# A tile's splits directly behind the next first layer, the inverse's halves ahead of the product, the row's square behind the second layer, and an earlier table

## The chip, the cores and the metric

The program runs on one core of one Trainium2 chip. The metric is the time on the device in microseconds (us). Five engines run their own queues in order: PE (TensorE; its weight loads are listed apart as PEld), DVE (VectorE), ACT (ScalarE), POOL (GpSimd) and SP (SyncE, which only issues DMAs here). An instruction that waits holds everything behind it on its own engine, and nothing on the others.

## What is computed

Cut to what matters, the reference is a chain of three layers over 8 x 3072 tokens of 256 features:

```python
y = irfft(rfft(x, axis=1) * F, n=3072)            # a long convolution, per feature
h = y @ w_in                                      # 256 -> 1024, the "first layer"
e = exp(h - max(h)); s = h * e / (sum(e) + 1e-9)  # the product h * e is "solu"
z = ((s - mean(s)) / sqrt(var(s) + 1e-6) * g_ln) @ w_out   # 1024 -> 256, the "second layer"
xn, en = z / (|z| + 1e-6), emb / (|emb| + 1e-6)
expert = argmax(xn @ en.T / tau); gate = softmax(xn @ en.T / tau)[expert]
out = gate * (relu(z @ w1[expert]) @ w2[expert])  # 8 experts, 256 -> 1024 -> 256
```

## The kernel before

**Stages.** The FFT is split as 64 x 48 over four passes of two batch rows each; its forward half (`fft`) runs one pass ahead of the rest. Stage B (`stage_b`) is a loop of 192 tiles of 128 tokens, 48 per pass, with the FFT of the next pass threaded through it as small units: `aux(.., 0)` behind the second layer, `aux(.., 1)` at the end of an iteration. In the last pass there is no FFT left, and the units split the expert weights instead (`w_split`, one ACT and one DVE instruction each). Stage C (`stage_c`) runs 128- or 256-token blocks of one expert each.

**What sets the order.** Nothing is reordered after it is written: each engine runs its instructions in the order in which the Python code issues them, with waits where data or a buffer asks for one.

**One iteration i of stage B**, in the order written, with j = i - 3:

- top: tile i-1 is split in two fp16 halves. Even tiles, and all 48 of the last pass, by `turn`: 8 transposes on PE (L936) write the tile's product `es` into its own first-layer PSUM tile `h`, ACT copies it to `T` (L939, the high half), DVE subtracts (L940, the low half). Odd tiles of the first three passes by `send`: ACT and DVE make the halves `hl` in place (L946, L947) and `post` sends them through a transposing DMA on SP one iteration later.
- ACT: `es` = exp (L967); DVE: the product `es` = h * cc * es (L968), which needs `cc` from POOL (L928, L929; the tiles are named `gcc`, `nm` and so on in the traces).
- even i: `inv4`, the fourth FFT stage, for two tiles: PE (L740) into a PSUM tile `a`, then its halves `xh` by ACT (L745) and `xl` by DVE (L746); both are written to the tile `xh`.
- `half`: last iteration's output rows, scaled by `c2` (ACT L1013, DVE L1014).
- the second layer of tile j: 24 matmuls (L983) into `o`.
- `aux(.., 0)`; the first layer of tile i+1 (L758, 12 matmuls); `top(i+1)`: DVE takes the maximum (L925) and `nm` (L926), POOL makes `cc`.
- ACT: the square of `es` into the junk tile `jk` (L995, for the variance); then the row's square, of `o` of tile j (L1001, for the norm), which POOL turns into `c2` (L1009).
- `aux(.., 1)`; then small steps of `b_final`, which routes a group of eight tiles to experts.

There are two `h` tiles in PSUM, so the first layer of tile i+1 overwrites the `h` of tile i-1 and has to wait until DVE's L940 of tile i-1 has read it. There are two `a` tiles, shared by the FFT units and `inv4`.

**Routing.** `b_final` runs a group's norm, softmax and positions as a generator, one step per iteration. Most groups are "slow": their long run of POOL operations (the loop of L808 to L811) is cut in several steps; the last groups run it in one go. One group's state (`snap`) is kept for an early table of the first 24 expert blocks (`first_slots`), whose first slot is gathered (L1169 on POOL) and transposed (L1174 on SP) before stage B ends.

## Time and profile before

| | us |
|---|---|
| median of 3 runs | 2745.77 (2744.71 to 2745.79) |
| the profiled execution | 2744.74 |
| its span, first to last instruction | 2742.9 |
| PE busy | 2620.9 (96%) |
| DVE busy | 1891.5 (69%) |
| ACT busy | 1527.3 (56%) |
| POOL busy | 1328.7 (48%) |

The busy times are over the whole span. Stage B lies between about 193 and 1683 us, stage C behind it. In the chain that ended last PE holds 39% and POOL 20% of the span. A wait in brackets behind a row is the idle time of that engine just before the instruction, with the instruction that ended it.

### The profile page before, as it was taken

How to read it: one execution, taken by the hardware profiler on the slowest of the kernel's cores; microseconds unless marked ns; L12 is line 12 of the kernel's file. 1: busy time of each engine (PE TensorE's matmuls, PEld its weight loads, DVE VectorE, ACT ScalarE, POOL GpSimd, SP SyncE). 2: the span in 40 equal slices, each digit the busy share in tenths (PEclk: the TensorE clock that was granted, in tenths of full speed). 3: DMA queues.
4: the chain of work that ended last, by engine and by line, in shares of the span. 5: the costliest groups of instructions: out<-in, count | busy, mean ns of one | idle time of the engine just before them, and what ended most of it. 6: DMA issues, size and time to landing. Idle time of an engine off the chain costs nothing.

```text
span 2742.9 us, 53684 instructions
## 1 busy us (share of the span) xinstructions
PE 2620.9 (96%) x20090; PEld 2024.3 (74%) x20090; DVE 1891.5 (69%) x2971; ACT 1527.3 (56%) x2852; POOL 1328.7 (48%) x2627
## 2 busy tenths in 40 slices
PE   5889999999999999999999998999999999999998
PEld 4447666676666776666776777888888888888897
DVE  4846899868989769888788975454545454454565
ACT  2556788767877767777688863223333333333332
POOL 2000346545566446665555556644444544454444
PEclk7999999999999999999999999999999999999999
DMA  9768888799997989885344422332323332322222
GB/s 313 202 193 244 222 199 199 195 246 209 195 194 161 234 222 198 191 169 138 94 122 122 126 51 56 74 76 73 79 74 78 76 76 77 77 77 76 78 60 57
DMA packets 444118, 384.13 MB, mean 140 GB/s; under 512 B 284779, under 2 KB 366837, under 8 KB 440784
## 3 DMA queue, kind: packets, MB, share of 16 engines
q1 hardware_dynamic: 391200, 310.34, 48.0%
q0 software_dynamic: 26896, 57.21, 6.8%
q10 hardware_dynamic: 25760, 13.14, 1.9%
q8 instruction: 159, 2.61, 0.4%
q14 instruction: 103, 0.84, 0.1%
HBM read 195.67 MB, written 103.09 MB: 109 GB/s over the span
## 4 chain that ended last, share of the span: by engine, by line
PE 39%; issue 23%; POOL 20%; DVE 12%; DMA 4%; ACT 1%; POOLq 0%; SPq 0%; ACTq 0%; DVEq 0%
PE h L758 15%; PE o L983 11%; POOL crow L1169 7%; POOL out_dram L166 6%; POOL scr L165 3%; DVE nm L925 3%; PE a L514 2%; PE a L688 2%; PE h L936 2%; PE a L740 2%; POOL gcc L928 2%; DMA bufA<-out 1%; DVE T L940 1%; DVE in L586 1%; PE a L650 1%
## 5 line engine op out<-in xcount | busy, mean ns | idle before, releaser
L983 PE MATMUL o<-wo_h,T 128*128 128x264 f16 x3072 | 549.6, 276 | 0.1
L928 POOL TENSOR_SCALAR gcc<-nm 128x1 f32<-128x1 f32 x192 | 180.3, 939 | 725.3 <-DVE nm L926 485.7
L758 PE MATMUL h<-win_h,xh 128*128 128x512 f16 x1536 | 492.4, 382 | 35.1 <-DVE T L940 33.5
L1212 PE MATMUL o<-cw,chh 128*128 128x256 f16 x3152 | 522.7, 273 | 0.8 <-issue 0.8
L1245 PEld LDWEIGHTS <-cw 128*128 128x128 f16 x5184 | 471.0, 98 | 58.1 <-issue 8.3
L983 PEld LDWEIGHTS <-T 128*128 128x128 f16 x4608 | 451.0, 98 | 64.4 <-ACT rows L1001 0.3
L758 PEld LDWEIGHTS <-xh 128*128 128x128 f16 x2304 | 222.0, 98 | 317.1 <-issue 84.8
L166 POOL DMA_INDIRECT out_dram<-cot,ids x197 | 215.2, 1092 | 452.9 <-ACT cot L1215 440.6
L1212 PE MATMUL o<-cw,chl 128*128 128x256 f16 x1576 | 429.7, 273 | 3.8 <-DVE chl L1249 3.6
L983 PE MATMUL o<-wo_l,T 128*128 128x264 f16 x1536 | 423.9, 276 | 0.0
L1249 DVE SCALAR_TENSOR_TENSOR chl<-h,chh 128x512 f16<-128x512 f32 x197 | 134.6, 683 | 389.9 <-ACT chh L1248 373.3
L925 DVE TENSOR_REDUCE nm<-h 128x1 f32<-128x1024 f32 x192 | 234.5, 1221 | 150.8 <-PE h L758 150.4
L1212 PEld LDWEIGHTS <-chh 128*128 128x128 f16 x3152 | 307.4, 98 | 36.7 <-issue 1.4
L1215 ACT ACTIVATE cot<-o,fac 128x256 f32<-128x256 f32 x197 | 93.5, 475 | 413.3 <-PE o L1212 407.6
L1201 DVE COPY cw<-wexp 128x4096 f16 x216 | 275.2, 1281 | 41.1 <-PE o L1212 20.7
L1245 PE MATMUL h<-cxT,cw 128*128 128x256 f16 (+1 forms) x2592 | 292.1, 264 | 7.2 <-DMA cxT<-crow 7.1
L758 PE MATMUL h<-win_l,xh 128*128 128x512 f16 x768 | 293.1, 382 | 0.0
L1245 PE MATMUL a<-cxT,cw 128*128 128x256 f16 (+1 forms) x2592 | 291.7, 263 | 0.4 <-issue 0.4
L968 DVE SCALAR_TENSOR_TENSOR es<-h,gcc,es 128x1024 f32<-128x1024 f32 x192 | 245.7, 1280 | 37.0 <-POOL gcc L929 31.9
L967 ACT ACTIVATE es<-h,nm,isc_h 128x1024 f32<-128x1024 f32 x192 | 230.2, 1199 | 31.3 <-DVE nm L926 19.4
L995 ACT ACTIVATE jk<-es 128x1024 bf16<-128x1024 f32 x192 | 202.1, 1052 | 64.2 <-DVE es L968 63.0
L166 POOL DMA_INDIRECT lst<-gdi,gix x192 | 218.1, 1136 | 35.3 <-issue 33.0
(261 smaller groups left out, 4368.7 us busy)
## 6 DMA issues: line engine op xcount, KB each, us to landing
wst<-in_w_dram SPq DMA_DIRECT2D x128, 256.0 KB
in<-in_x_dram SPq DMA_DIRECT2D x48, 512.0 KB
in<-bufA SPq DMA_DIRECT2D x64, 384.0 KB
c<-bufC SPq DMA_DIRECT2D x96, 256.0 KB
xs<-rows SPq DMA_DIRECT2D x96, 256.0 KB
ft<-in_filt_dram SPq DMA_DIRECT2D x24, 960.0 KB
bufA<-out SPq DMA_DIRECT2D x72, 256.0 KB
zw<-z SPq DMA_DIRECT2D x96, 192.0 KB
```

The lines of the kernel that those rows point to most:

```text
L166: ins = self.nc.gpsimd.indirect_dma_start(in_offset=None, **kw).ins
L758: nc.tensor.matmul(h[:, nb, :], l[:, i, db, :], r[:, db, sl], start=k == 0, stop=k == 5)
L925: nc.vector.tensor_reduce(x[:, 0:1], L["h"], axis=AX.X, op=ALU.max, negate=True)
L928: nc.gpsimd.tensor_scalar(cc, nm, nm, 1.0, op0=ALU.mult, op1=ALU.max)
L967: nc.scalar.activation(L["s"], L["h"], AF.Exp, bias=L["nm"], scale=self.isc_h[:, i // N2:i // N2 + 1], accum_out=col(i, "st", 0))
L968: nc.vector.scalar_tensor_tensor(L["s"], L["h"], col(i, "cc", 0), L["s"], op0=ALU.mult, op1=ALU.mult, accum_out=col(i, "st", 1))
L983: nc.tensor.matmul(o[:, :D + E], T[:, l, :], r[:, f, :], start=q == 0, stop=q == 23)
L995: nc.scalar.activation(jk, L["s"], AF.Square, accum_out=col(i, "st", 2))
L1169: nc.gpsimd.indirect_dma_start(out=rows[:, h, :], out_offset=None, in_=self.xs, in_offset=bass.IndirectOffsetOnAxis(ap=tab["ids"][:, h, k: ...
L1201: nc.vector.tensor_copy(w.rearrange("p (o k) -> p o k", o=1), self.wexp[:, bass.ds(e, 1), part * 4096:(part + 1) * 4096])
L1212: nc.tensor.matmul(o[:, :D], l[f // fs][:, f % fs, h * 128:(h + 1) * 128], w2[:, r, f, :], start=q == 0, stop=q == 23)
L1245: nc.tensor.matmul(t[:, i, :], w1[:, l, db, f * 128:(f + 1) * 128], xT[:, r + db, :n], start=q == 0, stop=q == 5)
```

## The change

Six edits in `stage_b`, and two in what goes with it:

1. `turn` and `send` of tile i move from the top of iteration i+1 to the end of iteration i, behind `jk` and ahead of `aux(.., 1)`. The tiles that go one way or the other stay the same.
2. `inv4`'s work of an even iteration is written ahead of the product L968 and behind the exponential.
3. The row's square and POOL's `c2` move directly behind the second layer, ahead of `aux(.., 0)`, the first layer and `jk`.
4. `first_slots` starts three iterations sooner, from tile 182 and no longer 185, on the state of group 19 and no longer 20; group 19 therefore runs its POOL operations in one go, too.
5. What is left of `b_final` in stage C stops once ahead of its matmul (the state 2), where it ran on before.
6. Two of the twelve transfer matrices that the FFT keeps from its first pass lie in buffers of the tag `wst` and no longer `mt`.

No arithmetic is added or removed, and no instruction: each engine has the same instructions before and after.

```diff
@@ -897,9 +897,7 @@
 
         def over(f, x):
 
-            while x in (2, 3):
-                x = next(f)
-            return x
+            return next(f) if x == 3 else x
 
         src = self.inv4(xp, ps)
         next(src)
@@ -959,17 +957,14 @@
         for i in range(n + LAG):
             j = i - LAG
             now = 0 <= i < n
-            if 0 <= i - 1 < n and i != n - 1:
-                (turn if i % 2 or i > n - N2 else send)(i - 1)
             if now:
                 L = live[i]
                 L["s"] = L["pool"].tile([128, FF], F32, name="es", tag="es")
                 nc.scalar.activation(L["s"], L["h"], AF.Exp, bias=L["nm"], scale=self.isc_h[:, i // N2:i // N2 + 1], accum_out=col(i, "st", 0))
-                nc.vector.scalar_tensor_tensor(L["s"], L["h"], col(i, "cc", 0), L["s"], op0=ALU.mult, op1=ALU.mult, accum_out=col(i, "st", 1))
-            if i == n - 1:
-                turn(i - 1)
             if i % 2 == 0:
                 xs.append(next(src, None))
+            if now:
+                nc.vector.scalar_tensor_tensor(L["s"], L["h"], col(i, "cc", 0), L["s"], op0=ALU.mult, op1=ALU.mult, accum_out=col(i, "st", 1))
             if half:
                 half()
                 half = None
@@ -984,6 +979,12 @@
                         q += 1
                 self.spot = o[:, 272:344]
                 finals = [(f, next(f) if x == 2 else x) for f, x in finals]
+                n2, c2 = col(j, "n2", 0), col(j, "cc", 1)
+                g, k = groups[j // G], j % G
+                if k % 2 == 0:
+                    rows = gp.tile([128, 2, RD], I32, name="rows", tag="rows", bufs=2)
+                nc.scalar.activation(rows[:, k % 2, :].bitcast(BF16)[:, :D], o[:, :D], AF.Square, accum_out=n2)
+                nc.gpsimd.tensor_scalar(c2.bitcast(I32), n2.bitcast(I32), -0.5, float(MAGIC + (8 << 23)), op0=ALU.mult, op1=ALU.add)
             if now:
                 if 0 < i <= n - N2 and i % 2 == 0:
                     post(i - 1)
@@ -993,12 +994,7 @@
                     top(i + 1)
                 jk = L["pool"].tile([128, FF], BF16, name="jk", tag="jk")
                 nc.scalar.activation(jk, L["s"], AF.Square, accum_out=col(i, "st", 2))
-            if 0 <= j < n:
-                n2, c2 = col(j, "n2", 0), col(j, "cc", 1)
-                g, k = groups[j // G], j % G
-                if k % 2 == 0:
-                    rows = gp.tile([128, 2, RD], I32, name="rows", tag="rows", bufs=2)
-                nc.scalar.activation(rows[:, k % 2, :].bitcast(BF16)[:, :D], o[:, :D], AF.Square, accum_out=n2)
+                (turn if i % 2 == 0 or i >= n - N2 else send)(i)
             if now:
                 aux(*divmod(i, N2), 1)
             if puts:
@@ -1006,7 +1002,6 @@
             if 0 <= j < n:
                 nc.vector.tensor_copy(g["raw"][:, k, :], o[:, D:D + E])
                 finals = [(f, next(f) if x == 3 else x) for f, x in finals]
-                nc.gpsimd.tensor_scalar(c2.bitcast(I32), n2.bitcast(I32), -0.5, float(MAGIC + (8 << 23)), op0=ALU.mult, op1=ALU.add)
 
                 def half(j=j, k=k, o=o, c2=c2, rows=rows):
                     rw = rows[:, k % 2, :].bitcast(F16)
@@ -1022,12 +1017,11 @@
 
                 if k == G - 1:
                     p, nn = divmod(j - (G - 1), N2)
-                    finals.append((self.b_final(groups.pop(j // G), p, nn, gp, ps, j // G == n // G - 4, j // G < n // G - 4), 0))
-            if i >= n - N2 + SPLIT + LAG:
+                    finals.append((self.b_final(groups.pop(j // G), p, nn, gp, ps, j // G == n // G - 5, j // G < n // G - 5), 0))
+            if i >= n - N2 + SPLIT:
                 next(early, 0)
             finals = [(f, x) for f, x in ((f, next(f, 1)) for f, _ in finals) if x != 1]
         self.spot = None
-        finals = [(f, over(f, x)) for f, x in finals]
         for _ in early:
             pass
         yield
@@ -1098,7 +1092,7 @@
         ins = nc.gpsimd.indirect_dma_start(
             out=li[:K].rearrange("p k o -> p (k o)"), out_offset=None, in_=self.lst.rearrange("(b k) o -> b (k o)", k=blk),
             in_offset=bass.IndirectOffsetOnAxis(ap=ri[:K].bitcast(U32), axis=0)).ins
-        assert len(self.scattered["lst"]) >= (self.np_run * N2 // G - (3 if start is None else 0)) * G
+        assert len(self.scattered["lst"]) >= (self.np_run * N2 // G - (4 if start is None else 0)) * G
         for name in self.scattered["lst"]:
             self.tc.add_manual_dep(ins, name, mybir.DependencyInfo(mybir.DependencyClass.Sync, mybir.DependencyReason.DATA), reason="the whole list")
         for _ in range(3 if start is None else 7):
@@ -1314,7 +1308,7 @@
                     self.m1 = [x[:, k:k + 4, :] for x in spare for k in (0, 4)]
                     for pool, tag in ((xp, "c4"), (xp, "xh"), (gp, "rows")):
                         self.m1 += [pool.tile([128, 4, 128], F32, name=tag, tag=tag, bufs=2) for _ in range(2)]
-                    self.m1 += [ap.tile([128, 4, 128], F32, name="mt", tag="mt", bufs=3) for _ in range(2)]
+                    self.m1 += [ap.tile([128, 4, 128], F32, name="wst", tag="wst", bufs=3) for _ in range(2)]
                     for _ in self.fft(0, ap, ps, hp):
                         next(prep, 0)
                     for _ in prep:
```

**DVE, an even tile of the second pass.** The rows below are DVE's queue around the product of tile 76. `nm` is the tile's maximum, `y` an FFT unit, `graw` the routing logits, `hl` the low half of tile 75, `xh` the low half of the inverse's output, `es` the product. Before:

```order
L925 TENSOR_REDUCE nm<-h 128x1
L926 TENSOR_SCALAR nm<-nm,isc_h 128x1
L600 TENSOR_TENSOR y<-z,ft 96x1024
L1007 COPY graw<-o 128x8
L947 TENSOR_TENSOR hl<-es,hl 128x1024
L968 SCALAR_TENSOR_TENSOR es,gst<-h,gcc,es 128x1024
L746 SCALAR_TENSOR_TENSOR xh<-a,ysc,xh 128x512
L1014 SCALAR_TENSOR_TENSOR rows<-o,gcc,rows 128x256
```

After:

```order
L923 TENSOR_REDUCE nm<-h 128x1
L924 TENSOR_SCALAR nm<-nm,isc_h 128x1
L945 TENSOR_TENSOR hl<-es,hl 128x1024
L600 TENSOR_TENSOR y<-z,ft 96x1024
L1003 COPY graw<-o 128x8
L746 SCALAR_TENSOR_TENSOR xh<-a,ysc,xh 128x512
L967 SCALAR_TENSOR_TENSOR es,gst<-h,gcc,es 128x1024
L1009 SCALAR_TENSOR_TENSOR rows<-o,gcc,rows 128x256
```

The low half of tile 75 moved from behind the FFT unit and the logits to directly behind `nm`, and the inverse's half from behind the product to ahead of it.

**DVE, the odd tile that follows.** `T` is the low half of tile 76; `gd`, `go`, `goh`, `grc` and `gy` are steps of `b_final`. Before:

```order
L925 TENSOR_REDUCE nm<-h 128x1
L926 TENSOR_SCALAR nm<-nm,isc_h 128x1
L608 TENSOR_TENSOR y<-y,zw 96x1024
L1007 COPY graw<-o 128x8
L840 SCALAR_TENSOR_TENSOR gd<-gd,cst 128x64
L842 TENSOR_REDUCE go_8494<-gd 128x8
L843 TENSOR_TENSOR goh<-gd,go_8494 128x64
L802 RECIPROCAL grc<-gcc 128x8
L803 TENSOR_SCALAR gy<-gV 128x16
L940 TENSOR_TENSOR T<-h,T 128x1024
L968 SCALAR_TENSOR_TENSOR es,gst<-h,gcc,es 128x1024
```

After:

```order
L923 TENSOR_REDUCE nm<-h 128x1
L924 TENSOR_SCALAR nm<-nm,isc_h 128x1
L938 TENSOR_TENSOR T<-h,T 128x1024
L608 TENSOR_TENSOR y<-y,zw 96x1024
L1003 COPY graw<-o 128x8
L840 SCALAR_TENSOR_TENSOR gd<-gd,cst 128x64
L842 TENSOR_REDUCE go_8505<-gd 128x8
L843 TENSOR_TENSOR goh<-gd,go_8505 128x64
L802 RECIPROCAL grc<-gcc 128x8
L803 TENSOR_SCALAR gy<-gV 128x16
L967 SCALAR_TENSOR_TENSOR es,gst<-h,gcc,es 128x1024
```

The low half of tile 76 moved ahead of the FFT unit, the logits and all steps of `b_final`.

**ACT, between the same two products.** `jk` is the square of the product, `rows,gn` the row's square, `z` and `out` are FFT copies, `T` is the high half of tile 76. Before:

```order
L651 ACTIVATE z<-a 96x512
L995 ACTIVATE jk,gst<-es 128x1024
L1001 ACTIVATE rows,gn_7975<-o 128x256
L695 ACTIVATE out<-a 96x512
L839 ACTIVATE gpe<-gd 128x64
L939 ACTIVATE T<-h 128x1024
L967 ACTIVATE es,gst<-h,nm,isc_h 128x1024
```

After:

```order
L986 ACTIVATE rows,gn_7978<-o 128x256
L651 ACTIVATE z<-a 96x512
L996 ACTIVATE jk,gst<-es 128x1024
L937 ACTIVATE T<-h 128x1024
L695 ACTIVATE out<-a 96x512
L839 ACTIVATE gpe<-gd 128x64
L963 ACTIVATE es,gst<-h,nm,isc_h 128x1024
```

The row's square went ahead of the FFT copy and of `jk`, and the high half ahead of the unit `out` and the exponential of `b_final`.

## Rows read from the trace of the kernel before

**Rows 1.** Busy time by stretch: us, length, then busy us of each engine, clock, DMA.

```profile
310.30:347.70 37.40, 33.98 (x204) 21.86 (x202) 33.17 (x46) 26.85 (x51) 11.77 (x26) 0.95 0.79 203
347.70:518.30 170.60, 164.89 (x1040) 108.51 (x1038) 158.08 (x248) 135.60 (x257) 97.44 (x201) 1.00 0.82 192
1392.50:1559.20 166.70, 160.99 (x1181) 117.59 (x1179) 147.36 (x270) 134.71 (x257) 90.75 (x259) 1.00 0.47 124
```

**Rows 2.** Whom PE waited for, whole span: total us, times, longest us.

```profile
PE h L758 <- DVE T L940: 33.5, 33, 2.9
...
PE h L1245 <- DMA cxT<-crow: 7.1, 1, 7.1
PE a L650 <- DVE xh L746: 4.4, 4, 2.1
PE a L514 <- DVE xh L746: 3.6, 3, 1.6
...
PE a L688 <- DVE xh L746: 3.1, 3, 1.2
...
PE a L851 <- DVE goh L843: 2.1, 1, 2.1
```

**Rows 3.** The same, from 193.5 to 1338.5 us alone.

```profile
PE h L758 <- DVE T L940: 24.6, 22, 2.9
```

**Rows 4.** Timeline around one wait: start us, us, engine, line, tiles.

```profile
811.13 1.03 ACT L939 ACTIVATE T<-h 128x1024 f16<-128x1024 f32 x1
...
812.04 0.21 DVE L926 TENSOR_SCALAR nm<-nm,isc_h 128x1 f32<-128x1 f32 x1
...
814.17 1.22 DVE L940 TENSOR_TENSOR T<-h,T 128x1024 f16<-128x1024 f32 x1
...
815.44 0.38 PE L758 MATMUL h<-win_h,xh 128*128 128x512 f16 x1 [0.79 <-DVE T L940]
```

**Rows 5.** Timeline: a slow POOL operation and what DVE ran meanwhile.

```profile
803.20 1.21 DVE L600 TENSOR_TENSOR y<-z,ft 96x1024 f32<-96x1024 f32 x1
...
803.39 2.40 POOL L928 TENSOR_SCALAR gcc<-nm 128x1 f32<-128x1 f32 x1 [1.96 <-DVE nm L926]
...
804.40 1.21 DVE L947 TENSOR_TENSOR hl<-es,hl 128x1024 f16<-128x1024 f32 x1
```

**Rows 6.** Groups by line: busy us, mean ns | idle us before them.

```profile
L968 DVE SCALAR_TENSOR_TENSOR es<-h,gcc,es 128x1024 f32<-128x1024 f32 x192 | 245.7, 1280 | 37.0 <-POOL gcc L929 31.9 <-ACT es L967 3.1
...
L1013 ACT ACTIVATE rows<-o,gcc 128x256 f16<-128x256 f32 x192 | 91.1, 475 | 52.4 <-POOL gcc L1009 43.5 <-POOL scr L165 7.9 <-DVE gpos L861 0.4
```

**Rows 7.** Timeline of an even tile of the last pass.

```profile
1375.64 0.71 ACT L462 ACTIVATE wexp<-wst,sc_w 128x512 f16<-128x512 f32 x1
...
1378.81 0.69 ACT L745 ACTIVATE xh<-a,ysc 128x512 f16<-128x512 f32 x1
...
1380.29 0.75 DVE L746 SCALAR_TENSOR_TENSOR xh<-a,ysc,xh 128x512 f16<-128x512 f32 x1
...
1382.92 1.04 PE L936 MATMUL h<-cst,es 128*128 128x128 f32 x8
```

**Rows 8.** Timeline: a product that waits for POOL, near the end of stage B.

```profile
1654.24 1.28 DVE L968 SCALAR_TENSOR_TENSOR es<-h,gcc,es 128x1024 f32<-128x1024 f32 x1 [2.98 <-POOL gcc L929]
...
1655.59 0.66 PE L936 MATMUL h<-cst,es 128*128 128x128 f32 x4 [1.36 <-DVE es L968]
```

**Rows 9.** Timeline: the start of stage C.

```profile
1679.75 1.23 DVE L1201 COPY cw<-wexp 128x4096 f16 x1 [1.08 <-DMA xs<-rows]
...
1683.67 0.58 PE L1245 MATMUL h<-cxT,cw 128*128 128x256 f16 x2 [7.08 <-DMA cxT<-crow]
...
1687.40 1.09 POOL L1169 DMA_INDIRECT crow<-xs,ids  x1 [2.37 <-DMA xs<-rows]
...
1696.13 1.03 PE L1245 MATMUL h<-cxT,cw 128*128 128x256 f16 x8
```

**Rows 10.** A stretch at half clock: columns as in the first group.

```profile
325.40:328.80 3.40, 3.40 (x10) 1.58 (x9) 0.88 (x2) 2.38 (x6) 0.00 (x0) 0.50 0.99 296
```


## The prediction

> **What bounds the kernel now.** I read busy time by stretch first, then whom PE waited for, then single stretches of the timeline. PE is busy for 2620.9 of the 2742.9 us, so nearly all that a reordering can give is PE's idle time, and the second question is whether the engine that PE waits for has time left. In stage C PE hardly waits, so what there is lies in stage B: in the long stretch of the second FFT pass PE is busy for 164.89 of 170.60 us and DVE for 158.08, in the last pass 160.99 and 147.36 of 166.70 [rows 1]. The list of PE's waits has one large entry: the first layer (L758) waited 33 times, 33.5 us in all, for L940, the low half that frees its `h` tile [rows 2]; 24.6 us of that lie in the three passes with an FFT [rows 3]. Three entries of 4.4, 3.6 and 3.1 us are FFT units that wait for DVE's `xl` (L746) to free an `a` tile. The start of stage C waited 7.1 us once, a matmul of `b_final` 2.1 us once [rows 2].
>
> **The low half behind the first layer.** The wait at 814 us shows how it arises [rows 4]. `nm` ends at 812.25, the high half on ACT at 812.16, so L940 could begin; but DVE first runs an FFT unit, the logits and five steps of `b_final`, and L940 runs from 814.17 to 815.39. PE was ready at 814.65 (815.44 less 0.79). After the change L940 stands behind `nm`: 812.25 + 1.22 = 813.47, 1.2 us before PE needs it. The 2 us of work that it passes come behind it and ahead of the same product, so the product starts when it did, and the new order takes nothing from the path there. What it costs is cover: where DVE is on time, it now idles behind `nm` until ACT has the high half, since the FFT unit no longer fills that gap. So the 33.5 us fall away at first order, and I ask how much DVE can honour. In the stretch from 310.3 it is busy for 33.17 of 37.40 us, and from 347.7 for 158.08 of 170.60 [rows 1]: for PE to lose its 5.7 us in the latter, DVE's idle time has to shrink from 12.5 to 6.8 us, while it gains small gaps behind `nm`. I let a third of the 24.6 us come back there (8.2) and a quarter of the other 8.9 (2.2). **Term: -33.5 + 10.4 = -23.1**, bounds -33.5 and -6.7 (all of the 24.6 back, with the 2.2).
>
> **The inverse's halves ahead of the product.** `xl` runs some 1.3 us sooner (the product ahead of it takes 1.28, [rows 6]), and the three waits for it are at most 2.1 us each. On DVE it also fills part of the 31.9 us in which the product waits for POOL's `gcc` [rows 6]. The 11.1 us go but for 2. **Term: -9**, bounds -11.1 and -5. Against it stands the product, which now ends later on even tiles: `xl` needs ACT's `xh`, and that stands behind the exponential. In the last pass [rows 7] `xh` ends at 1379.50; a weight split of 0.71 us that ACT ran ahead of the high half now runs behind it and ahead of the exponential, so 1380.2; `xl`, which ran behind the product from 1380.29, takes 0.75 and the product 1.28 [rows 6], so the product ends at 1382.2. The transposes of that tile begin at 1382.92. They have 0.7 us to spare, and less where DVE comes late. **Term: +2** for tiles where it isn't enough, bounds 0 and +6.
>
> **The transposes** themselves stand ahead of an FFT unit (in the FFT passes) that used to cover a late product; in the rows of tile 76 the order changes by that one unit and PE's total doesn't. At nothing, with the term above as the price if the cover was needed.
>
> **The row's square behind the second layer.** ACT waited 43.5 us in all for `c2` before it scaled the rows (L1013, [rows 6]), because POOL held `c2` behind the next tile's `gcc`. It now has it an iteration's half earlier. ACT is not what PE waits for, so I count 0; ACT in turn may wait for the second layer with `jk` and the high half queued behind, but both need later work of DVE and PE anyway. SP's queue keeps its order here.
>
> **The early table.** One more group runs its POOL operations in one go. The one near the end shows the price: the product waited 2.98 us for `gcc` and the transposes on PE 1.36 [rows 8]. **+1.4**, bounds 0 and +3. The gain is at the start of stage C [rows 9]: the first block waited until 1683.67 for its transposed rows, which now land three iterations sooner. The weights of that block are the next to be late: their copy began at 1679.75 and took 1.23, so PE could start at 1681.0, 2.7 us sooner, more if that copy moves up. But the second block's gather on POOL began only at 1687.40, when the last rows had landed, and its matmuls began at 1696.13; if these rows are not written sooner, the gain ends in a wait there. POOL no longer runs the first gather between two `c2`, so they should be. On SP the first block's two transposes pass two writes of rows, which wait no longer for it than before. **-2.5**, bounds 0 and -7.1.
>
> **The rest.** The stop ahead of the matmul in stage C gives DVE time for `goh`: **-2.1** at best, 0 at worst; I take -2. The granted clock showed 0.50, its lower level of 1.2 GHz, from 325.4 to 328.8, [rows 10], right behind one of the 33 waits for L940; 3.4 us at half speed are 1.7 us of work. If that wait goes, they go: **-1.7**, or 0. The two matrices in other buffers I count at 0: what stands behind them in the first pass waits for other transfers.
>
> **Sum.** -23.1 - 9 + 2 + 1.4 - 2.5 - 2 - 1.7 = -34.9 against the profiled execution's own 2744.74, which gives 2709.8. The median of the runs is 1 us above that execution, less than anything decided here: 2710. All bounds on one side give 2689, on the other 2742.
>
> **A rule that speaks against it.** At 803.39 POOL's `gcc`, an operation on 128 x 1 elements, took 2.40 us, just as long as DVE ran an FFT unit and the low half of `hl` back to back [rows 5]. The Trainium skill (SBUF — State Buffer, section SBUF: two separate sides) says that a DVE instruction with two inputs in SBUF and a GpSimd one that reads SBUF exclude each other for a whole instruction. These rows agree. `hl` now directly follows the `nm` that also releases `gcc`, so by that rule POOL would lose that race on all 72 tiles that go by `hl`; `T` reads PSUM and SBUF and would not hold it.
>
> **Rivals.** *DVE stays late* (0.16): `gcc` loses 1.2 us (the `hl` row, [rows 5]) on each of the 72 `hl` tiles, `xl` covers 0.75 of it, and 0.45 x 72 = 32 us of DVE's time are gone where it has 5 to 12% left. This is what the rule above would do. Then the waits in the FFT passes return in full and only 8.9 - 2.2 of the first term, -9, +2, +1.4, -2.5 and -2 remain: -16.8, so 2728. Against it: the old order had an FFT unit or `hl` there already. *Everything goes* (0.12): no give-back, no late product: -33.5 - 11.1 - 2.7 - 2.1 - 1.7 + 1.4 = -49.7, so 2695, and 2691 if the start of stage C gives all of its wait. *Slower* (0.06): the product on even tiles. It decides at the 0.7 us of [rows 7]: if `xh` comes 1.2 us later than I place it, on the 24 even tiles of the last pass and the 72 of the others, transposes wait 0.5 us 96 times, +48, and the time is 2758. Against it: in the FFT passes the product of an even tile already waits for `gcc`, which `xl` fills. *It does not do what it says* (0.04): L940 is bound by the high half, not by its place, and the time stays within 4 us of 2744. In [rows 4] the high half was done before `nm`, which speaks against it.
>
> **How the numbers follow.** The forecast has 0.62, around 2710 from about 2695 to 2724. The range of 2690 to 2732 holds nearly all of it, most of "DVE stays late" and most of "everything goes"; slower, no effect and their edges, some 0.2, are left out. About 0.2%, 5.5 us, is what a measurement of this kernel can tell from no change: faster by more 0.90, within it 0.04, slower 0.06.
>
> **What would show it.** Right: the wait of the first layer for L940's successor falls from 33.5 to about 10 us, the waits of FFT units for `xl` below 3, ACT's wait for `c2` to a few us, the first block of stage C starts 3 to 4 us behind the last second layer. Wrong: a new entry of transposes that wait for the product of more than 6 us, the product's wait for `gcc` above 45 us, or a second block of stage C that waits for its rows. The prediction fails if DVE's idle time in the FFT passes does not shrink: then PE's waits only change their name.

## The result, and the profile of the changed kernel

The changed kernel took 2708.37 us (median of 4 runs, 2706.89 to 2717.36) against 2745.78 for the kernel before beside it; the ratio is 0.9865, with a 95% interval of 0.9839 to 0.9892. The forecast was 2710.

| | before | after |
|---|---|---|
| the profiled execution, us | 2744.74 | 2717.36 |
| its span, us | 2742.9 | 2715.5 |
| PE busy, us | 2620.9 | 2617.8 |
| DVE busy, us | 1891.5 | 1888.3 |
| POOL busy, us | 1328.7 | 1290.6 |

The profiled execution of after is the longest of its four, and 7 us of what sets it apart arise before 240 us, in the start-up: up to there its PE was busy for 186.52 us, in a second profile of the same kernel (span 2707.2) for 193.23. I therefore compare stretches behind 240 us rather than ends.

Most of the gain is PE's idle time in stage B. Busy time from 240 to 1600 us (columns as in [rows 1]), first the kernel before, then after:

```profile
240.00:1600.00 1360.00, 1317.15 (x8768) 914.77 (x8767) 1154.93 (x1947) 1036.58 (x1966) 736.51 (x1778) 1.00 0.77 179
```

```profile
240.00:1600.00 1360.00, 1342.68 (x8992) 929.51 (x8991) 1178.11 (x2013) 1056.22 (x2006) 709.81 (x1818) 1.00 0.79 181
```

PE stands idle for 17.3 us instead of 42.9. DVE is busy for 23 us more of the same stretch, since the changed kernel gets further in it; over the whole span it is busy for about as long as before. POOL is busy for 27 us less, though it has the same instructions; one operation, `gcc` (below), takes less time. Whom PE waits for now, whole span (answers [rows 2]; L938 is the former L940, L934 the transposes, L967 the product, L1239 stage C's first matmuls):

```profile
PE a L514 <- ACT out L515: 23.1, 6, 7.7
...
PE h L934 <- DVE es L967: 7.4, 10, 1.7
...
PE h L1239 <- issue: 3.1, 1, 3.1
PE h L1239 <- DMA cxT<-crow: 3.1, 2, 2.6
...
PE o L851 <- DVE goh L843: 2.6, 3, 1.5
PE a L650 <- DVE xh L746: 2.5, 3, 0.9
...
PE a L688 <- DVE xh L746: 2.1, 2, 1.5
...
PE h L758 <- DVE T L938: 1.5, 2, 0.9
```

The transposes' entry of the kernel before, which [rows 2] leaves out:

```profile
PE h L936 <- DVE es L968: 2.3, 2, 1.4
```

The first layer's 33.5 us are 1.5, the FFT units' 11.1 us for `xl` are 4.6, and the transposes' 2.3 us for the product are 7.4. The largest entry, L514, lies in the start-up.

The groups that answer [rows 6] (L1008 is the former L1013), then `gcc`, the low half and `xl`, columns as there; the last two rows are `gcc` and the low half of the kernel before:

```profile
L967 DVE SCALAR_TENSOR_TENSOR es<-h,gcc,es 128x1024 f32<-128x1024 f32 x192 | 243.4, 1268 | 9.4 <-ACT es L963 4.4 <-issue 2.5 <-POOL scr L165 2.1
L926 POOL TENSOR_SCALAR gcc<-nm 128x1 f32<-128x1 f32 x192 | 124.6, 649 | 602.4 <-DVE nm L924 602.1
L1008 ACT ACTIVATE rows<-o,gcc 128x256 f16<-128x256 f32 x192 | 91.1, 474 | 64.6 <-DVE graw L1003 28.8 <-DVE gpos L861 11.5 <-POOL gt L804 5.1
L938 DVE TENSOR_TENSOR T<-h,T 128x1024 f16<-128x1024 f32 x120 | 146.5, 1221 | 34.6 <-ACT T L937 32.9 <-ACT jk L996 1.7
L746 DVE SCALAR_TENSOR_TENSOR xh<-a,ysc,xh 128x512 f16<-128x512 f32 x96 | 71.7, 747 | 45.5 <-ACT xh L745 40.3 <-issue 2.2 <-ACT es L963 1.7
...
L928 POOL TENSOR_SCALAR gcc<-nm 128x1 f32<-128x1 f32 x192 | 180.3, 939 | 725.3 <-DVE nm L926 485.7 <-DVE graw L1007 235.4 <-DVE pm_x L265 4.0
L940 DVE TENSOR_TENSOR T<-h,T 128x1024 f16<-128x1024 f32 x120 | 144.6, 1205 | 20.4 <-ACT T L939 20.4
```

The product's 31.9 us of waiting for `gcc` have left the row. DVE now waits 40.3 us for ACT's `xh` instead, ahead of the product. ACT's 43.5 us for `c2` are gone, but ACT still stands idle for 64.6 us ahead of its scaled rows, 28.8 of it behind `graw`.

One odd and one even tile of the second pass, timeline of after (answers [rows 4, 5]):

```profile
800.50 0.21 DVE L924 TENSOR_SCALAR nm<-nm,isc_h 128x1 f32<-128x1 f32 x1
800.63 1.22 DVE L938 TENSOR_TENSOR T<-h,T 128x1024 f16<-128x1024 f32 x1
...
800.83 0.31 POOL L926 TENSOR_SCALAR gcc<-nm 128x1 f32<-128x1 f32 x1 [1.44 <-DVE nm L924]
...
807.33 1.22 DVE L945 TENSOR_TENSOR hl<-es,hl 128x1024 f16<-128x1024 f32 x1
...
807.52 2.25 POOL L926 TENSOR_SCALAR gcc<-nm 128x1 f32<-128x1 f32 x1 [3.26 <-DVE nm L924]
...
808.46 1.22 DVE L600 TENSOR_TENSOR y<-z,ft 96x1024 f32<-96x1024 f32 x1
...
810.49 0.75 DVE L746 SCALAR_TENSOR_TENSOR xh<-a,ysc,xh 128x512 f16<-128x512 f32 x1 [0.73 <-ACT xh L745]
811.15 1.27 DVE L967 SCALAR_TENSOR_TENSOR es<-h,gcc,es 128x1024 f32<-128x1024 f32 x1
811.29 1.10 PE L688 MATMUL a<-y,cst 96*96 96x512 f32 x2 [0.64 <-DVE xh L746]
```

At 800.63 the low half starts as soon as `nm` is done; at 814 us of the kernel before [rows 4], 2 us of other work stood in between. `gcc` takes 0.31 us beside it. On the even tile `gcc` takes 2.25, as long as `hl` and the FFT unit together; the product starts behind `xl` all the same, for `xl` waited 0.73 us for `xh`.

### The profile page after: what moved, and what is told of

Same layout as the page of the kernel before. It is cut to its first block, busy times and chain, and to the rows that moved or that the text cites. A ratio compares the mean times of both kernels' runs of the same rounds, so it can differ in the third digit from the quotient of the medians.

```text
span 2715.5 us, 53743 instructions
## 1 busy us (share of the span) xinstructions
PE 2617.8 (96%) x20090; PEld 2016.0 (74%) x20090; DVE 1888.3 (70%) x2971; ACT 1528.3 (56%) x2852; POOL 1290.6 (48%) x2627
## 4 chain that ended last, share of the span: by engine, by line
PE 46%; issue 21%; POOL 16%; DVE 9%; DMA 4%; ACT 3%; POOLq 0%; SPq 0%; DVEq 0%; ACTq 0%
PE h L758 14%; PE o L978 14%; POOL crow L1163 6%; POOL out_dram L166 6%; PE h L934 3%; POOL scr L165 3%; PE a L688 3%; PE a L514 3%; PE a L740 2%; PE o L1206 2%; DVE es L967 2%; DMA bufA<-out 1%; PE a L650 1%; DVE nm L923 1%; PE h L1239 1%
## 5 line engine op out<-in xcount | busy, mean ns | idle before, releaser
L1239 PEld LDWEIGHTS <-cw 128*128 128x128 f16 x5184 | 471.6, 98 | 58.5 <-issue 7.8
L926 POOL TENSOR_SCALAR gcc<-nm 128x1 f32<-128x1 f32 x192 | 124.6, 649 | 602.4 <-DVE nm L924 602.1
L1195 DVE COPY cw<-wexp 128x4096 f16 x216 | 274.6, 1278 | 40.9 <-PE o L1206 20.4
L1239 PE MATMUL h<-cxT,cw 128*128 128x256 f16 (+1 forms) x2592 | 292.5, 264 | 6.3 <-issue 3.1
L1239 PE MATMUL a<-cxT,cw 128*128 128x256 f16 (+1 forms) x2592 | 292.8, 264 | 0.6 <-issue 0.6
L967 DVE SCALAR_TENSOR_TENSOR es<-h,gcc,es 128x1024 f32<-128x1024 f32 x192 | 243.4, 1268 | 9.4 <-ACT es L963 4.4
L1163 POOL DMA_INDIRECT crow<-xs,ids x197 | 201.3, 1022 | 64.4 <-issue 62.9
```

Source lines behind the costliest of these rows:

```text
L967: nc.vector.scalar_tensor_tensor(L["s"], L["h"], col(i, "cc", 0), L["s"], op0=ALU.mult, op1=ALU.mult, accum_out=col(i, "st", 1))
L1163: nc.gpsimd.indirect_dma_start(out=rows[:, h, :], out_offset=None, in_=self.xs, in_offset=bass.IndirectOffsetOnAxis(ap=tab["ids"][:, h, k: ...
L1195: nc.vector.tensor_copy(w.rearrange("p (o k) -> p o k", o=1), self.wexp[:, bass.ds(e, 1), part * 4096:(part + 1) * 4096])
L1239: nc.tensor.matmul(t[:, i, :], w1[:, l, db, f * 128:(f + 1) * 128], xT[:, r + db, :n], start=q == 0, stop=q == 5)
```

## The experiments

Several chips ran them. The kernel before took 2736.95 us beside the first four kernels, 2743.16 beside the next four, 2741.70 beside the ones with `hl` and with the logits and 2739.19 beside the ones with the steps alone and without the early table, so ratios to it are compared; a difference in us is the ratio's on 2745.8. "PE idle" is PE's idle time from 240 to 1600 us of the profile, as above.

| kernel | ratio, 95% interval | us against before | PE idle, us |
|---|---|---|---|
| before | | | 42.9 |
| splits alone | 0.9919, 0.9905 to 0.9932 | -22.2 | 24.6 |
| inverse's halves alone | 0.9958, 0.9944 to 0.9971 | -11.5 | 32.2 |
| row's square alone | 1.0011, 1.0001 to 1.0021 | +3.0 | 44.1 |
| table and stop alone | 0.9987, 0.9978 to 0.9996 | -3.6 | 43.2 |
| the change again | 0.9857, 0.9842 to 0.9872 | -39.3 | 16.1 |
| without the low half's new place | 0.9945, 0.9931 to 0.9958 | -15.1 | 33.9 |
| without the inverse's halves | 0.9883, 0.9868 to 0.9899 | -32.1 | 22.3 |
| without the row's square | 0.9885, 0.9869 to 0.9901 | -31.6 | 20.6 |
| without `hl`'s new place | 0.9866, 0.9851 to 0.9881 | -36.8 | 16.2 |
| without the early table | 0.9876, 0.9857 to 0.9895 | -34.0 | 15.2 |
| logits and steps behind the product | 1.0351, 1.0330 to 1.0372 | +96.4 | 96.0 |
| steps alone behind the product | 0.9872, 0.9854 to 0.9890 | -35.1 | 21.3 |

**The splits alone.** The theory was that of the prediction, the rivals that the wait comes back under another name or not at all.

```diff
-            if 0 <= i - 1 < n and i != n - 1:
-                (turn if i % 2 or i > n - N2 else send)(i - 1)
...
             if now:
+                (turn if i % 2 == 0 or i >= n - N2 else send)(i)
                 aux(*divmod(i, N2), 1)
```

> The kernel before with the first edit alone: the splits of tile i (transposes, high half, low half, or the two halves for the transposing DMA) at the end of iteration i. Theory of the prediction: the first layer's wait for the low half falls from 33.5 to about 10 us, and the clock's dip at 325 us goes with it: -23.1 - 1.7, so 2721 us, ratio 0.991. Rival A, the time comes back on DVE: that wait changes its name (the maximum or the product comes late), -9 at most, 2737 us or more. Rival B, nothing comes back: -33.5 - 1.7, 2711 us or less, and then nearly the whole gain of 37 us is this edit's.

Measured -22.2 us (-26.1 to -18.7), so the theory's size holds, between both rivals. Its place doesn't. Whom PE waits for in this kernel (L936 are the transposes, L966 the product):

```profile
PE h L936 <- DVE es L966: 6.1, 8, 1.3
PE a L688 <- DVE xh L746: 4.9, 3, 2.3
...
PE a L740 <- ACT out L695: 3.3, 3, 1.4
...
PE h L758 <- DVE T L940: 1.5, 2, 0.9
```

The first layer's wait falls to 1.5 and not to 10. What comes back does so elsewhere: waits for `xl` 15.2 us (11.1 before, with L650 at 7.3 and L514 at 3.0), transposes 6.1 (2.3), L740 3.3 for an FFT copy that ACT now runs behind the high half (none among the waits before): together 11 us. The clock's dip did not go with the wait, either: the granted clock is at 0.50, its lower level of 1.2 GHz, near 327 us here too, right behind a wait of 2.31 us for `xl` (columns as in [rows 1]):

```profile
327.30:330.60 3.30, 3.30 (x9) 1.05 (x8) 3.27 (x4) 1.99 (x5) 0.00 (x0) 0.50 0.74 204
```

**The inverse's halves alone.**

```diff
+            if i % 2 == 0:
+                xs.append(next(src, None))
             if now:
                 nc.vector.scalar_tensor_tensor(L["s"], ...)
             if i == n - 1:
                 turn(i - 1)
-            if i % 2 == 0:
-                xs.append(next(src, None))
```

> The kernel before with the second edit alone: the inverse's halves ahead of the product. Theory of the prediction: three waits for the low half of the inverse shrink from 11.1 to 2 us and the product on even tiles costs 2: -7, so 2739 us, ratio 0.997. Rival, read from the profile of the changed kernel, where those waits fell only to 4.6 and the transposes' wait for the product rose by 5.1: -6.5 + 5.1 = -1.4, within 0.2% of no change. If it is slower by 5 us or more, the product is what suffers.

Measured -11.5 (-15.4 to -8.0): more than either expected. In its profile the waits for `xl` hold 1.4 us (11.1 before), the first layer's 31.5 (33.5) and the transposes' 3.4 (2.3), and PE's idle time is 10.7 us less. The rival, read off the whole change, had charged this edit with lateness that the splits bring.

```profile
PE h L936 <- DVE es L971: 3.4, 3, 1.3
...
PE a L514 <- DVE xh L746: 1.2, 2, 0.6
...
PE a L650 <- DVE xh L746: 0.2, 1, 0.2
```

**The row's square alone.**

```diff
                 finals = [(f, next(f) if x == 2 else x) for f, x in finals]
+                (the row's square on ACT, c2 on POOL)
...
-                (the row's square on ACT)
...
-                (c2 on POOL)
```

> The kernel before with the third edit alone: the row's square on ACT and its c2 on POOL directly behind the second layer. Theory of the prediction: ACT's wait of 43.5 us for c2 goes, and PE's waits stay, since ACT is not what PE waits for: 0, so 2746 us. Rival A: c2 now stands ahead of the next tile's gcc on POOL and the product no longer waits 31.9 us for gcc, and what comes sooner on DVE takes a third of the first layer's 33.5 us: -11, 2735 us. Rival B: ACT waits for the second layer with the high half queued behind it, and the time grows by 3 us or more.

Measured +3.0 (0.3 to 5.8). ACT's wait for `c2` fell from 43.5 to 5.8 us and the product's for `gcc` only from 31.9 to 28.3, so rival A is out; PE's idle time is 1.2 us more. That ACT is not what PE waits for held as far as that profile shows. Rival B, a loss of 3 us or more, is not excluded by the time, though PE's idle time speaks for less.

**The early table and the stop alone.**

```diff
-... j // G == n // G - 4, j // G < n // G - 4
+... j // G == n // G - 5, j // G < n // G - 5
-            if i >= n - N2 + SPLIT + LAG:
+            if i >= n - N2 + SPLIT:
...
-        finals = [(f, over(f, x)) for f, x in finals]
```

(and `over` as in the change.)

> The kernel before with the fourth and fifth edits alone: the early table three iterations sooner on group 19, and the stop ahead of the matmul in stage C. Theory of the prediction: -2.5 at the start of stage C, -2 for the matmul, +1.4 for the burst on POOL: -3.1, so 2743 us, ratio 0.9989. Rival, read from the profile of the changed kernel: the first block's wait of 7.1 us becomes 3.1 + 2.6 with a second one for the rows of the second block, and the matmul's 2.1 us come back elsewhere: within 2 us of no change.

Measured -3.6 (-6.0 to -1.1), near the theory's -3.1, though the interval reaches into the rival's 2 us. Its start of stage C (L1242 is the first layer there):

```profile
PE h L1242 <- issue: 3.1, 1, 3.1
...
PE h L1242 <- DMA cxT<-crow: 1.7, 3, 1.0
```

Of the 1.7 us only the longest wait, 1.0, lies at the start of stage C, for the second block; the others come at 2625 and 2710 us. So it is 4.1 us in place of 7.1, and the matmul's 2.1 us for `goh` don't stand among the waits any more. The +1.4 for POOL does not show: the transposes wait 2.0 us here and 2.3 before.

**The change again,** as a control for the next three kernels.

> The changed kernel itself, beside the kernel before on this chip and beside the next three. If the four edits add up as they stand alone (ratios 0.9919, 0.9958, 1.0011 and 0.9987), the ratio is 1 - 0.0081 - 0.0042 + 0.0011 - 0.0013 = 0.9875; a ratio under 0.984 would mean that they help each other, one over 0.990 that they stand in each other's way.

0.9857, and 0.9865 in the first comparison. The sum of the single edits, 0.9875, lies 0.0003 above the interval of the second, inside that of the first, and has an error of its own: the edits add up, or help each other a little. The sixth edit, the two matrices in other buffers, was not run alone; that it costs and gives nothing is not shown.

**The low half back at its old place,** the rest of the change kept.

```diff
-            nc.vector.tensor_tensor(lo, h, hi, op=ALU.subtract)
+            M["lo"] = lambda: nc.vector.tensor_tensor(lo, h, hi, op=ALU.subtract)
...
             now = 0 <= i < n
+            if i > 0 and i - 1 in live:
+                live[i - 1].pop("lo", int)()
```

> The changed kernel with DVE's low half of T alone put back to the top of the next iteration, behind the FFT unit, the logits and the steps of the routing; the transposes on PE and the high half on ACT stay at their new place. Theory: it is the place on DVE that counts, so the first layer's wait returns to 30 us or more and the time rises by 18 to 25 us over the changed kernel, ratio to before about 0.995. Rival: the transposes and the high half, which now stand sooner, are what let the low half come in time; then it stays within 5 us of the changed kernel.

It lies 0.0088 above the control, 24.2 us, and the wait is back, though transposes and high half stand at their new place:

```profile
PE h L758 <- DVE T L938: 25.9, 23, 3.1
...
PE h L934 <- DVE es L969: 4.4, 3, 2.0
```

So it is the place on DVE, though the wait stays below the 30 us of the theory. It is 25 us more than in the control, but other waits shrink: the transposes' from 7.4 to 4.4, those for `xl` from 5.2 to 1.5. PE's idle time from 240 to 1600 us grows by 17.8 us; the rest of the 24.2 these rows do not account for.

**The inverse's halves back behind the product,** the rest kept (the edit of the second kernel, backward).

> The changed kernel with the inverse's halves put back behind the product. Theory, the edits add up: the FFT units' waits for the low half of the inverse return from 4.6 to 15 us as in the kernel with the splits alone, the transposes wait 1 to 2 us less, and the time rises by 9 to 12 us, ratio to before about 0.991. Rival: in the whole change the product suffers from standing behind it (DVE waits 40 us for the high half of the inverse), so putting it back costs 3 us at most, or gains.

0.0026 above the control, 7.1 us, though the intervals overlap; the theory's 9 to 12 us were too much. The waits tell more: for `xl` 14.6 us (three entries, the first shown) against 5.2 in the control's profile, the transposes 5.3 against 7.4.

```profile
PE a L650 <- DVE xh L746: 7.3, 4, 2.6
PE h L934 <- DVE es L964: 5.3, 8, 1.2
```

So in the whole change this edit takes 9.4 us away and costs 2.1 at the transposes, as the prediction's -9 and +2 have it; the difference, 7.3 us, is about the 7.1 of the time.

**The row's square back,** the rest kept.

> The changed kernel with the row's square and its c2 put back behind the junk square. Theory, the edits add up: alone this edit gave a ratio of 1.0011, so without it the time stays or falls by up to 3 us, ratio to before 0.985 to 0.9875. Rival: in the whole change it is what takes the product's wait for gcc from 21.5 us (with the splits alone) to nearly nothing, so without it the product comes late, the transposes wait 5 us more, and the time rises by 4 us or more, ratio 0.989.

0.0028 above the control, 7.7 us, with intervals that overlap. The rival named the cost but not the reason: the product's wait for `gcc` is 2.6 us, the transposes' 7.3 as before. What differs are L740's wait for an FFT copy of ACT, 2.3 against 1.0, and L688's for `xl`, 4.0 against 2.1. PE's idle time gives 4.5 us of the 7.7. So the waits speak for a use of this edit beside the splits, and the kernel with it alone shows none without them; by the time alone it stays open, and of the size I can only say 0 to 8 us.

**`hl` back at its old place,** the edit of "the low half back", but for `send` and not for `turn` (its second part, at the top of the iteration, is the same).

```diff
-            nc.vector.tensor_tensor(hl[:, 1, :], M["s"], hl[:, 0, :], op=ALU.subtract)
+            M["lo"] = lambda: nc.vector.tensor_tensor(hl[:, 1, :], M["s"], hl[:, 0, :], op=ALU.subtract)
```

> The changed kernel with DVE's low half of hl (odd tiles of the first three passes) alone put back to the top of the next iteration; all else stays. In the changed kernel POOL's gcc takes 1.22 us on these 72 tiles and 0.30 on the other 120, since hl now runs on DVE while gcc is ready. Theory: that does not reach PE, and hl is not what the gain came from, so the time stays within 4 us of the changed kernel, ratio to before 0.985 to 0.9875. Rival, DVE and POOL in each other's way cost time here: with hl later gcc ends sooner on odd tiles, the product comes sooner, and the time falls by 5 us or more, ratio 0.984 or less.

0.9866: no difference, as the theory had it. `gcc` doesn't end sooner either: on the 72 tiles in question it takes 1.46 us here and 1.22 in the changed kernel (means of the trace), since the FFT unit, and not `hl`, now follows `nm`.

**Logits and steps behind the product.** An attempt to do better than the change.

```diff
-            if 0 <= j < n:
-                nc.vector.tensor_copy(g["raw"][:, k, :], o[:, D:D + E])
...
-            finals = [(f, x) for f, x in ((f, next(f, 1)) for f, _ in finals) if x != 1]
+            def tail(...):    # the same lines
+            tails.append(tail)
...
                 (the product)
+            if tails:
+                tails.pop()()
             if half:
```

> The changed kernel with the logits, the steps of the routing and those of the early table (from the copy to graw to the end of the iteration) written behind the next tile's product and ahead of the scaled rows. Theory: these steps, now between the splits and the product, are what makes the product late for the transposes, mostly on odd tiles of the last pass; their wait falls from 7.4 to 3 us or less and the time by 3 to 5 us, ratio to before about 0.984. Rival: DVE's time is only moved; the scaled rows and the tile that the second layer writes come later by as much, and the time stays within 2 us of the changed kernel or grows.

It is 96 us slower than the kernel before. The theory is out, and the rival, which allowed for growth, had no such size in it. ACT's scaled rows and whom PE waits for:

```profile
L1014 ACT ACTIVATE rows<-o,gcc 128x256 f16<-128x256 f32 x192 | 90.9, 473 | 390.1 <-DVE graw L1009 287.0 <-DVE gpos L861 42.4 <-POOL gu L791 17.5
```

```profile
PE h L758 <- DVE T L940: 38.5, 45, 1.8
PE a L740 <- ACT out L695: 16.8, 21, 1.8
...
PE a L740 <- ACT z L651: 12.2, 14, 1.5
PE o L851 <- DVE goh L843: 11.5, 4, 3.8
```

ACT's scaling waits for DVE's copy of the logits out of the same tile `o`. That copy now stands behind the product, so of the 390 us that ACT stood idle ahead of the scaling 287 ended with that copy and 42 with `gpos`, a routing step that reads `o` too; FFT copies and high halves were queued behind. All of them only read `o`. The Trainium skill (PSUM — Partial Sum Buffer, section PSUM bank collisions raise a hardware error) says why they may not run at once: two engines at the same time on the same 32 partitions of one PSUM bank collide, reads against reads included, and the compiler puts a dependency between two such instructions. The trace shows the wait that goes with it, not the collision.

**The steps alone behind the product,** the copy and the steps that read `o` left where they were.

```diff
+            if i > n - N2 + SPLIT:
+                next(early, 0)
+            finals = [(f, x) for f, x in ((f, next(f, 1)) for f, _ in finals) if x != 1]
             if half:
...
-            if i >= n - N2 + SPLIT:
-                next(early, 0)
-            finals = [(f, x) for f, x in ((f, next(f, 1)) for f, _ in finals) if x != 1]
```

> The changed kernel with only the later steps of the routing and those of the early table written behind the next tile's product; the copy of the logits and the steps that read the second layer's tile stay where they are, since ACT's scaled rows stood 287 us behind that copy when it was moved too. Theory: that copy was the whole cost of the former kernel, so this one is back within 4 us of the changed kernel, ratio to before 0.984 to 0.987, and the transposes wait 1 to 2 us less. Rival: the steps themselves, late by a product, hold up POOL's gcc or the matmuls of the routing on PE (11.5 us in the former kernel), and it is 10 us or more slower than the changed kernel, ratio 0.990 or more.

0.9872: back at the changed kernel's time, at the edge of the theory's range, so the loss came from the copy and the steps that read `o`, which stayed in place here; the two were not parted. No gain either: the routing's matmul waits 9.0 us for `goh`, and the transposes 7.2, not 1 to 2 us less.

**Without the early table,** the stop kept (the fourth edit backward).

> The changed kernel with the early table put back to tile 185 and group 20; the stop ahead of the routing's matmul in stage C stays. Theory, from the fourth and fifth edits alone (ratio 0.9987): the first block of stage C waits 7 to 8 us for its transposed rows again instead of 3.1, the second block's wait of 1.5 to 2.6 us goes, and the time rises by 2 to 4 us, ratio 0.987. Rival: with the rest of the change the rows are written sooner, the start of stage C is no later than with the early table, and the time stays within 1 us or falls, since one group fewer runs its POOL operations in one go.

0.9876, 0.0019 above the control of another chip, with intervals that overlap: by time it stays open. By the waits the rival is wrong, for the first block waits again:

```profile
PE h L934 <- DVE es L967: 10.1, 13, 2.0
...
PE h L1239 <- DMA cxT<-crow: 6.6, 2, 6.4
```

6.4 us there (the other 0.2 come at 2597 us) in place of 3.1 + 1.5 in the control: 2 us. The transposes wait 2.7 us more than in the control, which I had not expected of the later table. 1.0 us of that the control lists under "issue", and most of the rest is one tile, 189, whose product waits for POOL here and not in the control:

```profile
1617.52 1.28 DVE L967 SCALAR_TENSOR_TENSOR es<-h,gcc,es 128x1024 f32<-128x1024 f32 x1 [3.01 <-POOL gcc L927]
...
1618.87 1.09 PE L934 MATMUL h<-cst,es 128*128 128x128 f32 x8 [1.46 <-DVE es L967]
```

With the later table the product waits for POOL at tiles 181 and 189, as in the kernel before; with the earlier one, in the control, only at tile 173 of the last pass. Why is open.

No version beat the change by more than these runs can tell.

## Why the prediction was right, step by step

The total was right, 2710 against 2708, and so was the largest term. Nevertheless two of its three signs of "wrong" came true (the transposes' 7.4 us and a second block that waits for its rows), and two of the four of "right" did not come as written: the first layer's wait fell to 1.5 us and not to about 10, and the waits for `xl` to 4.6 and not below 3. So the terms have to be gone through. That the total came out so close is partly luck: the square gave more than the 0 it was counted at as far as the waits tell, the clock's -1.7 has no ground, and the late product cost more.

- **The low half, -23.1.** Right in size: -22.2 alone, and 24.2 lost when it is undone. In the working, the 10.4 us that were let come back at the first layer are wrong as to the place: only 1.5 us stayed there. The 11 us that came back lie at `xl`, the transposes and L740; that 11 is close to 10.4 is luck, since the shares of a third and a quarter came from no row. DVE did shrink its idle time as the condition asked: 240 to 1600 us hold 23 us more of its work. In the long stretch from 347.7 us its idle time went from 12.5 to 9.2 us, though, and not to the 6.8 that the working asked for.
- **`xl`, -9 and +2.** -11.5 alone; in the whole -9.4 and +2.1 by the waits. Right. The reading that the product's 31.9 us for `gcc` would be filled is right too: [rows 6]'s entry is gone, and 22.3 of it return when `xl` goes back.
- **The late product, +2 (0 to +6).** Mis-sized as a total: the transposes wait 5.1 us more. The step that failed is "so the product starts when it did". The working saw that DVE would idle behind `nm` until ACT has the high half, but let that come back at the first layer. This idle time grew from 20.4 to 32.9 us, it stands ahead of the product, and the transposes, whose own move was put at nothing, had lost the cover for a late product. It was not the even tiles of the last pass, to which [rows 7] gave 0.7 us to spare. Of the ten waits one, 1.67 us, is at the first tile, four are at even tiles of the FFT passes (0.20 to 0.73 us each) and five at odd tiles of the last pass, where every tile has transposes: 151, 159, 173, 183 and 191 (0.41 to 1.22). The splits alone bring 3.8 of the 5.1, the inverse's halves alone 1.1. With the low half back at its old place, only the first tile, 173 and 191 wait. Tile 151 in after, with the last steps of a group on DVE:

```profile
1363.85 0.25 POOL L871 TENSOR_SCALAR ggate<-ggate 128x8 f32<-128x8 f32 x1 [2.57 <-DVE ggate L870]
1364.14 0.20 DVE L874 RECIPROCAL grg<-ggate 128x8 f32<-128x8 f32 x1 [0.38 <-POOL ggate L871]
...
1364.26 1.23 DVE L967 SCALAR_TENSOR_TENSOR es<-h,gcc,es 128x1024 f32<-128x1024 f32 x1
...
1365.56 0.66 PE L934 MATMUL h<-cst,es 128*128 128x128 f32 x4 [0.41 <-DVE es L967]
```

  DVE waits for POOL in the middle of the routing's steps, and, ahead of these rows, 0.45 us for the high half before the low half; the product pays both. Tile 159 has the same rows. At tile 173 it is POOL: the product waits for it for 2.11 us and the transposes 1.22. That the low half's place makes tiles 151, 159 and 183 late is shown by the kernel that undoes it; how the two idle times share in it is argued from the timeline.
- **Table and stop, -2.5, +1.4 and -2.** -3.6 alone against -3.1. The start of stage C gave 3.0 alone, and the second block waited for its rows (1.0 alone, 2.6 and 1.5 in the two profiles of the change), as the text feared. The first block's 3.1 us have no releaser in the row; DVE's copy of that block's weights ends at 1650.61 us of after and PE starts at 1650.71, so it is the weights, which the working named as the next to be late. The +1.4 has the wrong sign by the waits: one more group in one go on POOL brought no further wait, and without the early table the transposes wait at one tile more. The stop is mixed: its wait is gone alone, but the same matmul waits 2.6 us in the profile of after and 1.2 in the second one, at three and two places in the last pass.
- **The row's square, 0.** Alone between nothing and a small loss; beside the splits a gain by the waits, not clear of noise by the time. The step "ACT is not what PE waits for" is not true any more once the high half stands ahead of ACT's FFT copies: L740 then waits for one of these, 3.3 us with the splits alone.
- **The clock, -1.7.** Not tied to the low half. With the splits alone the dip stayed, at 327 us. In the second profile of the changed kernel the granted clock still fell to 0.50, its lower level of 1.2 GHz, near 330 us, right behind a wait of 1.50 us for `xl`; in the first profile the same wait took 1.49 us, at 333.67, and the clock stayed at 1.00.
- **The rivals.** "DVE stays late" built on POOL losing the race on the 72 `hl` tiles. It does: `gcc` takes 1.22 us on these and 0.30 on the other 120 (means of the trace of after; the rows at 800.83 and 807.52 are one of each). By the Trainium skill (SBUF — State Buffer, section Who interferes with whom) a DVE instruction with two SBUF inputs gets in the way of a GpSimd one that reads SBUF, and one with at most one SBUF input, such as the low half that reads PSUM, does not; the trace agrees on both. But its price never came, because FFT units had held `gcc` before: the same 72 took 1.46 us each and the other 120 took 0.63, 180.3 us in all against 124.6 now. With `hl` back at its old place they took 1.46 us again and the time did not change. "Slower" fell since the late tiles are ten and not 96.

## What to carry to other kernels

A step that frees a buffer for the busiest engine belongs directly behind what it needs, ahead of work that nobody waits for soon; here it ended 32 us of waiting at the first layer, and 22 us were left as a gain, since 11 us of other waits came in their place. What comes back shows up at whatever now stands behind it on the same queues, so the units of work that were passed should be listed by who waits for them, on ACT too and not on DVE alone. And before a small copy is moved, ask which engine's queue waits for it: moving one of 0.16 us, with the steps that read the same tile, cost the whole gain and 96 us more.

## What the runs showed of the hardware

The start-up ahead of stage B differed by 7 us between two profiles of one kernel (PE busy 186.52 and 193.23 of the first 240 us), and the kernel before took 2736.95 to 2745.78 us in different comparisons. Differences of a few us between kernels of separate comparisons are therefore read from waits and not from times here. PE's fall to half clock isn't fixed to a kernel either: in one profile of the changed kernel it came near 330 us, behind a wait of 1.50 us, and in the other there is none between 240 and 1600 us, though the same wait, 1.49 us, is there. So a wait ahead of a fall is not shown to be its cause.
